# Other steps for the last-stage chunks, the weight scalings and half of block 0's last down products in a fused spectral filter and MLP

## The chip, the cores and the metric

The kernel runs on one core of one Trainium2 chip. The metric is device time in microseconds (us) from start to end of the program. TensorE (PE in the profile) does the matrix products, VectorE (DVE) and ScalarE (ACT) the elementwise work, GpSimd (POOL) some sums and its own DMA queue, SyncE (SP) most DMA issues. Each engine works through its own list in order and waits on semaphores for the others.

## The reference

For each of 8 batches, a sequence of 3008 tokens of width 256 is filtered in the frequency domain; then all 24064 tokens go through a two-layer MLP with a hard-swish between the layers, everything in float32:

```python
X = np.fft.rfft(x, axis=1)
Y = X * (filt_r + 1j * filt_i)[None]
y = np.fft.irfft(Y, n=3008, axis=1).reshape(24064, 256)
h = y @ w_in                      # 256 -> 2048
g = h * np.clip(h + 3, 0, 6) / 6
out = g @ w_out                   # 2048 -> 256
```

## The kernel before, in words

**The MLP is the frame.** The 24064 tokens are cut into 47 blocks of 512, held as 256 pairs (a sum half and a difference half of two tokens). Each block `k` takes 8 steps, `p` = 0 to 7, one for each 256 of the 2048 hidden columns. A step is numbered s = 8k + p. From block 1 on, both layers use a seven-product scheme (Strassen-like) on 2 by 2 blocks: a step has seven up products (`product`, L681) and the seven down products of the step before (`down`, L757), fourteen in place of sixteen. Block 0 uses plain products (`plain_up` L789, `plain_down` L800).

**The order inside a step** is written out by hand in the loop at L1093. TensorE gets: `up_1` (products A11, S1, A12), the step's early extra work, down 1, `up_2` (S2, S4), down 2 and 4, `up_3` (S3), down 5 and 6, `up_5` (A22), down 7 and 3. The two accumulators `al` and `be` in PSUM are used again and again: A22 needs `al` free, that is after VectorE's L712 has read it. ScalarE copies `al` and `be` out (L692, L693, L702, L721) and does two relus a step (`relu`, L726). VectorE does, in this order, the second hard-swish of the step before (`hswish(.., 1)`, L731), three sums of it (`g_sums`, L738, L739, L741), the additions L707 and L712, and the first hard-swish of the step (L731). At p = 0 of a block the outputs of the block before are collected (`out_1` on ScalarE, `out_2`, `out_3` on VectorE); at p = 1 follow `out_4` (two VectorE additions, L832 and L833, and one on GpSimd, L834) and `out_5` (L837), then the stores.

**The Fourier stages of later batches are placed into the steps of earlier blocks** by a plan: `at(step, fn, ...)` puts a function into a step. Functions of the tuple `EARLY` run right after `up_1`, all others at the end of the step. There are four stages: `a_unit` (first stage), `b_unit`, `f_unit`, `y_unit` and `bi_unit` (second stage: transform, multiplication with the filter on VectorE in L508 to L510, combination on VectorE in L519 and L520, inverse), and the last stage, `n_unit` and `n_five`. `n_five` takes a chunk of five frequencies of 47 pairs, 80 small matmuls (L621) into two PSUM tiles of the pool `psF`, which has just two buffers and serves all four stages. Then ScalarE copies them into the ring `xn` (L603), and if the chunk completes a block's 256 pairs, `ready` calls `t_sums`: seven GpSimd additions (L677) that make that block's `xt`, the inputs of its up products.

**Kinds of blocks.** For batch n from 2 on, the six blocks from `first[n] - 7` on get the letters c a A B A B. In blocks A and B the second stage runs: `f_unit` at steps 2, 3, 6, 7 of A and 4, 5 of B; `y_unit` at 4 and 5 of A and 2, 3, 6, 7 of B; `bi_unit` at 0 and 6 of B and at step 1 of the second A and of the block behind the last B. `FIVE_AT` says in which step of block k - 1 a chunk that begins in block k is made: for a block that holds the start of only one chunk, 4 in A, 2 in B. The DMA load of a chunk's inputs, `t4_load`, is placed one step behind the chunk that used the same half of the buffer.

**Block 1's weights.** Its sums of weight blocks are made on GpSimd (`w_sums`, L361) and two of them, S1 and A22, are multiplied by 2 and -2 in place by ScalarE (`w_scale`, L365), for p in step 7 + p, one step before `up_1` and `up_5` of block 1 use them.

**The end of block 0.** `plain_down` of p = 7 is done in step 8 (block 1, p = 0): sixteen matmuls between `up_4` and `up_5`, then `plain_out`, two ScalarE copies (L807) and the stores.

Of the kernel before, what the change touches and what calls it, by code (L numbers as in the profile page):

```python
# [33 lines left out]
D = 256  # L34
B = 8
# [146 lines left out]
def kernel(  # L182
# [482 lines left out]
    def xb(k, d, c):  # L665
        return xn[:, d, c, ts(k % 3, PAIRS)]
# [13 lines left out]
    def product(ps, p, w, x, start=False, stop=False):  # L680
        nc.tensor.matmul(ps, w_in[p][:, w, :], x, start=start, stop=stop, skip_group_check=True)  # L681
# [32 lines left out]
    def up_4(k, p):  # L714
        st["g", k, p] = gp.tile([P, 7, 256], FP32, name="g")
        relu(0)

    def up_5(k, p):
        al = st["up"][0]
        product(al, p, A22, xb(k, 1, 1), stop=True)  # L720
        nc.scalar.activation(out=st["h"][1][:, 0:256], in_=al, func=AXT.Copy)  # L721
        relu(1)

    def relu(i):
        r = rp.tile([P, 512], FP32, name="r", tag="r")
        nc.scalar.activation(out=r, in_=st["h"][i], func=AXT.Relu, bias=half_c, scale=1.0 / 6.0)  # L726
        st["r", i] = r
# [6 lines left out]
    def g_sums(k, p):  # L734
        hswish(k, p, 1)
        g = st["g", k, p]
        v = nc.vector
        v.tensor_tensor(out=g[:, G1, :], in0=g[:, G3, :], in1=g[:, G22, :], op=ALU.add)  # L738
        v.tensor_tensor(out=g[:, G3:G2 + 1:2, :], in0=g[:, G3:G1 + 1, :],  # L739
                        in1=g[:, G11:G11 + 1, :].broadcast_to([P, 2, 256]), op=ALU.subtract)  # L740
        v.tensor_tensor(out=g[:, G4, :], in0=g[:, G12, :], in1=g[:, G2, :], op=ALU.subtract)  # L741
# [19 lines left out]
    def last_down():  # L761
        p, v, add = NP - 1, nc.vector.tensor_tensor, ALU.add
        g, o = st["g", LAST, p], st["o", LAST][0]
        hswish(LAST, p, 1)
        ps = [psF.tile([P, 512], FP32, name="psf", tag="f") for t in range(2)]
        for i, a in ((0, G11), (1, G12)):
            for t in range(2):
                for u in range(2):
                    nc.tensor.matmul(ps[t][:, ts(u, D)], g[:, a + t, ts(u, P)],
                                     w_out[p][:, 2 * i:2 * i + 2, :].rearrange("p j m -> p (j m)"),  # L770
                                     start=i == 0 and u == 0, stop=i == 1, skip_group_check=True)
        out_4(LAST)
        v(out=o_at(LAST, 0, 1), in0=st["po", LAST][3][:, 1, :, :], in1=o_at(LAST, 0, 1), op=add)
        for t, qs in ((0, (nc.sync, nc.gpsimd, nc.scalar)), (1, (nc.sync, nc.scalar))):
            both = o[:, t, :, :].rearrange("p u d -> p (u d)")
            v(out=both, in0=ps[t], in1=both, op=add)
            store_last(t, qs)
# [6 lines left out]
    def plain_up(p):  # L784
        st["g", 0, p] = gp.tile([P, 7, 256], FP32, name="g")
        st["h"] = [psU.tile([P, 512], FP32, name=n) for n in ("al", "be")]
        for i in range(2):
            for d in range(2):
                nc.tensor.matmul(st["h"][i], w_in[p][:, 2 * d + i, :], xn[:, d, :, 0:PAIRS], start=d == 0, stop=d == 1)  # L789
            relu(i)  # L790
            hswish(0, p, i)

    def plain_down(p):
        g = st["g", 0, p]
        if p == 0:
            st["po", 0] = [psO.tile([P, 2, 2, P], FP32, name="po%d" % i) for i in range(2)]
        for t in range(2):
            for u in range(2):
                for i, a in ((0, G11), (1, G12)):
                    nc.tensor.matmul(st["po", 0][t][:, u, :, :].rearrange("p a m -> p (a m)"), g[:, a + t, ts(u, P)],  # L800
                                     w_out[p][:, 2 * i:2 * i + 2, :].rearrange("p j m -> p (j m)"),
                                     start=p == 0 and u == 0 and i == 0, stop=p == NP - 1, skip_group_check=True)

    def plain_out():
        st["o", 0] = op.tile([P, 2, 2, D], FP32, name="o", tag="o"), None
        for t, po in enumerate(st.pop(("po", 0))):
            nc.scalar.activation(out=st["o", 0][0][:, t, :, :].rearrange("p u d -> p (u d)"),  # L807
                                 in_=po.rearrange("p a u m -> p (a u m)"), func=AXT.Copy)
        store(0)
# [49 lines left out]
    def store(k):  # L859
        o = st["o", k][0]  # L860
        nc.sync.dma_start(o_d[ds(k * PAIRS, PAIRS)].rearrange("(u p) d -> p u d", p=P), o[:, 1, :, :])
        for u, p, m, b_, j, a in runs(k):
            for h in range(1 if j else 2):
                nc.sync.dma_start(raw(out, b_ * N + row(j, h, a), [[NC * D, m], [1, D]]), o[p:p + m, h, u, :])
        for b_, r, j, m, na in BACK.get(k, ()):
            to, half = out.offset + (b_ * N + N - j) * D, D // 2
            a0, a1 = ([[D, m], [-NC * D, na], [1, D]], [[NA * D, m], [D, na], [1, D]]) if m > 1 else (
                [[half, 2], [-NC * D, na], [1, half]], [[half, 2], [D, na], [1, half]])
            nc.sync.dma_start(bass.AP(tensor=out.tensor, offset=to, ap=a0),
                              bass.AP(tensor=o_d.tensor, offset=o_d.offset + r * D, ap=a1))  # L870
# [13 lines left out]
    plan = {}  # L884


    EARLY = (a_unit, b_unit, bi_unit, n_unit, n_five)

    def at(step, fn, *a):
        plan.setdefault((step, fn in EARLY), []).append((fn, a))  # L890

    with tc.manual_schedule():

# [113 lines left out]
        for i in range(2 * NP):  # L1007
            at(min(6 + i // 2, NP + 2), w_sums, i, int(i == gate), 4)
# [6 lines left out]
        n_at = {0: -2, 1: -2}  # L1015
        kinds = {}
        for n in range(2, B):
            for d, kind in enumerate("caABAB"):
                kinds[first[n] - 7 + d] = kind

        N_AT = {"c": ((6, 6), (3, 3), (6, 6)), "a": ((2, 4), (2, 4), (6, 6)), "A": ((4, 5), (1, 1), (4, 5)), "B": ((2, 3), (1, 1), (2, 3))}
        FIVE_AT = {"c": (6, 3, 6), "a": (4, 2, 4), "A": (4, 0, 4), "B": (2, 1, 3)}
        N_FIRST = {0: ((3, 4),), 1: ((), (2, 2), (3, 3)), 2: ((1, 1),), 3: ((1, 1),)}
        in_block = {}
        for i in range(2, len(chunks)):
# [2 lines left out]
        for i in range(2, len(chunks)):  # L1028
# [3 lines left out]
            at_, kind = same.index(i) + 1 if len(same) > 1 else 0, kinds.get(k - 1, "a")  # L1032
            steps = N_FIRST[k - 1][at_] if k - 1 in N_FIRST else (FIVE_AT[kind][at_],) * 2 if len(chunks[i][1]) == NJ else N_AT[kind][at_]
            if head and len(same) == 1:
# [58 lines left out]
        for i in range(len(items) + 1):  # L1093
            up = i < len(items)
            k, p = items[min(i, len(items) - 1)]
            dn = i > 0
            kd, pd = items[i - 1]
            def do(early):
                for fn, a in plan.get((i, early), ()):
                    fn(*a)  # L1100

            if k == 0:
                plain_up(p)
                do(True)
                if dn:
                    plain_down(pd)
                do(False)
                continue
            if not up:
                last_down()  # L1110
                break
            up_1(k, p)
            ends = k == LAST and p == NP - 1
            do(True)
            last_plain = dn and kd == 0
            dn = dn and kd > 0
            if dn:
                g_sums(kd, pd)
                down(kd, pd, 1)
            if up:  # L1120
                up_2(k, p)
            if dn and pd == 0 and kd > 1:
                out_4(kd - 1)
            if up:
                up_2b(k, p)
            if dn:
                down(kd, pd, 2, 4)
                if pd == NP - 1:
                    out_1(kd)
            if up:  # L1130
                up_3(k, p)
            if dn:
                down(kd, pd, 5, 6)
            if up:
                up_4(k, p)
            if ends:
                out_1(k)
            if last_plain:
                plain_down(pd)
                plain_out()  # L1140
            if dn and pd == 0 and kd > 1:
                out_5(kd - 1)
            if up:
                hswish(k, p, 0)
            if up:
                up_5(k, p)
            if dn:
                if pd == NP - 1 or ends:
                    out_2(kd)
                down(kd, pd, 7, 3)  # L1150
                if pd == NP - 1 or ends:
                    out_3(kd)
            do(False)


# [28 lines left out]
```

## Time and profile before

| what | value |
|---|---|
| median of 3 runs | 2675.4 us (2675.08 to 2677.41) |
| the profiled execution's own time | 2675.01 us |
| span in the profile | 2673.2 us |
| PE busy | 2646.0 us, 99% |
| DVE busy | 2064.2 us, 77% |
| ACT busy | 1303.9 us, 49% |
| POOL busy | 510.3 us, 19% |
| granted clock | 0.999 |

The times between the starts of the first product (A11) of one step and of the next, from the timeline:

| steps | length, us |
|---|---|
| with the up and down products only (146 of 169) | 6.15 |
| with `n_five` (29 of 45) | 7.66 |
| with `a_unit` (48 of 49) | 7.37 |
| with `bi_unit` of step 1 in the second A, or with `b_unit` | 7.36 to 7.37 |
| step 4 of A, with `n_five` (12) | 7.75 to 7.76 |
| step 5 of A, products only (12) | 6.87 to 6.89 |
| step 3 of B, products only (9) | 6.87 to 6.88, once 7.10 |
| steps 8 to 15 (block 1) | 8.85, 7.90, 8.03, 8.23, 7.38, 7.38, 6.52, 7.38 |

Busy shares are averages over the whole span. The modelled ends of matmuls make PE look busy where it waits, so a wait is better seen in the length of a step.

### The profile page before, as it was taken

Reading aid. Unit: us, or ns where it says so; the run is one execution under the profiler, and the core shown is the slowest. Engines: PE = TensorE matmul, PEld = TensorE weight load, DVE = VectorE, ACT = ScalarE, POOL = GpSimd, SP = SyncE. Lnnn points to the kernel's source line nnn. Section 1 sums busy time; section 2 is a strip of 40 time slices with the busy share of each in tenths; the row PEclk is TensorE's granted clock in tenths of the full one; section 3 lists DMA queues with packets and bytes.
Section 4 is the critical chain, followed back from the end, with each engine's and each line's share of the span. In section 5 each row is a group of like instructions: output and inputs, shape, how many; then the busy total and the mean of one; then the engine's idle time right before and its main releaser. Section 6 shows DMA issues by size and latency. Waiting matters only on the chain.

```text
span 2673.2 us, 54258 instructions
## 1 busy us (share of the span) xinstructions
PE 2646.0 (99%) x21584; PEld 2316.2 (87%) x21584; DVE 2064.2 (77%) x3503; ACT 1303.9 (49%) x2672; POOL 510.3 (19%) x731
## 2 busy tenths in 40 slices
PE   9999999999999999999999999999999999999999
PEld 6588888888888888888888888888888888899998
DVE  7978867887678876788767887678886888767666
ACT  4444444445444445445454545545445454454554
POOL 2242122111221112211131111311112111111110
PEclk9999999999999999999999999999999999999999
DMA  9732233212332123311233112231123321110000
GB/s 255 206 95 70 61 105 96 64 38 66 90 103 61 41 65 88 109 56 40 70 84 109 56 41 75 79 108 56 41 74 79 108 59 39 52 42 18 23 20 24
DMA packets 134818, 198.24 MB, mean 74 GB/s; under 512 B 23146, under 2 KB 99016, under 8 KB 134374
## 3 DMA queue, kind: packets, MB, share of 16 engines
q1 hardware_dynamic: 117037, 150.12, 19.8%
q0 software_dynamic: 16960, 44.16, 6.3%
q8 instruction: 170, 2.79, 0.4%
q14 instruction: 82, 0.67, 0.1%
q10 hardware_dynamic: 569, 0.50, 0.1%
HBM read 122.43 MB, written 83.98 MB: 77 GB/s over the span
## 4 chain that ended last, share of the span: by engine, by line
PE 89%; DVE 9%; issue 1%; ACT 1%; DMA 0%; POOL 0%; SPq 0%; DVEq 0%; POOLq 0%; ACTq 0%
PE po L757 40%; PE al L681 22%; PE be L681 17%; PE psn L621 2%; PE psf L531 2%; PE psf L440 2%; DVE g L731 2%; PE psf L487 1%; DVE y L519 1%; DVE y L520 1%; DVE g L738 1%; DVE h L707 1%; DVE h L712 1%; DVE g L739 1%; DMA w_all<-in_x_dram 0%
## 5 line engine op out<-in xcount | busy, mean ns | idle before, releaser
L757 PEld LDWEIGHTS po<-w_all,g 128*128 128x128 f32 x10276 | 1361.2, 191 | 154.6 <-issue 44.1
L757 PE MATMUL po<-w_all,g 128*128 128x128 f32 x10276 | 1402.6, 277 | 0.4 <-DVE g L731 0.2
L726 ACT ACTIVATE r<-h,half_c 128x512 f32<-128x512 f32 x736 | 531.0, 721 | 362.9 <-DVE h L707 350.8
L731 DVE SCALAR_TENSOR_TENSOR g<-r,h 128x512 f32<-128x512 f32 x736 | 526.9, 716 | 209.5 <-ACT r L726 195.7
L681 PE MATMUL al<-xt,w_all 128*128 128x256 f32 x2208 | 659.8, 381 | 0.8 <-POOL w_all L361 0.6
L681 PE MATMUL be<-xt,w_all 128*128 128x256 f32 x1472 | 437.9, 379 | 0.0
L707 DVE TENSOR_TENSOR h<-be,s 128x512 f32<-128x512 f32 x368 | 253.8, 690 | 167.3 <-PE be L681 162.6
L681 PEld LDWEIGHTS al<-xt,w_all 128*128 128x128 f32 x2208 | 335.3, 192 | 1.9 <-POOL w_all L361 1.5
L681 PEld LDWEIGHTS be<-xt,w_all 128*128 128x128 f32 x1472 | 279.7, 190 | 37.8
L721 ACT ACTIVATE h<-al 128x256 f32<-128x256 f32 x368 | 141.0, 383 | 326.8 <-PE al L681 326.8
L712 DVE TENSOR_TENSOR h<-al,s 128x256 f32<-128x256 f32 x368 | 155.7, 423 | 154.3 <-PE al L681 153.1
L739 DVE TENSOR_TENSOR g<-g 128x512 f32<-128x512 f32 x367 | 255.6, 696 | 12.6
L677 POOL TENSOR_TENSOR xt<-xn 128x256 f32<-128x256 f32 x184 | 145.3, 809 | 539.7 <-ACT xn L603 539.7
L702 ACT ACTIVATE s<-al 128x256 f32<-128x256 f32 x368 | 141.1, 383 | 194.9 <-PE al L681 191.3
L681 PE MATMUL al<-xn,w_all 128*128 128x256 f32 x736 | 222.5, 384 | 10.4 <-DVE h L712 10.4
L693 ACT ACTIVATE s<-be 128x256 f32<-128x256 f32 x368 | 141.1, 383 | 178.6 <-PE be L681 178.6
L681 PE MATMUL be<-xn,w_all 128*128 128x256 f32 x736 | 219.7, 380 | 1.0 <-ACT w_all L365 0.5
L738 DVE TENSOR_TENSOR g<-g 128x256 f32<-128x256 f32 x367 | 172.3, 469 | 12.5
L547 POOL DMA_DIRECT2D g_tmp<-t x96 | 55.4, 591 | 656.7 <-ACT t L534 644.3
L692 ACT ACTIVATE s<-al 128x256 f32<-128x256 f32 x368 | 140.9, 383 | 68.5 <-PE al L681 68.5
L741 DVE TENSOR_TENSOR g<-g 128x256 f32<-128x256 f32 x367 | 160.0, 436 | 12.5
L461 POOL DMA_DIRECT2D z_tmp<-t x192 | 95.1, 503 | 364.6 <-DVE t L454 347.4
(149 smaller groups left out, 1867.3 us busy)
## 6 DMA issues: line engine op xcount, KB each, us to landing
g_tmp<-t POOLq DMA_DIRECT2D x96, 256.0 KB, 3.7
t<-g_tmp SPq DMA_DIRECT2D x184, 120.0 KB
t<-z_tmp SPq DMA_DIRECT2D x42, 512.0 KB
z_tmp<-t POOLq DMA_DIRECT2D x192, 96.0 KB, 2.5
xs<-in_x_dram SPq DMA_DIRECT2D x112, 128.0 KB
o_tmp<-o SPq DMA_DIRECT2D x46, 256.0 KB
ft<-in_filt_r_dram SPq DMA_DIRECT2D x168, 64.0 KB
ft<-in_filt_i_dram SPq DMA_DIRECT2D x168, 64.0 KB
```

The lines of the kernel that those rows point to most:

```text
L677: nc.gpsimd.tensor_tensor(out=o, in0=x0, in1=x1, op=op_)
L681: nc.tensor.matmul(ps, w_in[p][:, w, :], x, start=start, stop=stop, skip_group_check=True)
L693: nc.scalar.activation(out=s5, in_=be[:, 1, :], func=AXT.Copy)
L702: nc.scalar.activation(out=s[:, 1, :], in_=al, func=AXT.Copy)
L707: nc.vector.tensor_tensor(out=st["h"][0].rearrange("p (a n) -> p a n", a=2), in0=be, in1=s, op=ALU.add)
L712: nc.vector.tensor_tensor(out=st["h"][1][:, 256:512], in0=al, in1=s5, op=ALU.add)
L726: nc.scalar.activation(out=r, in_=st["h"][i], func=AXT.Relu, bias=half_c, scale=1.0 / 6.0)
L731: nc.vector.scalar_tensor_tensor(out=st["g", k, p][:, o:o + 2, :].rearrange("p a n -> p (a n)"), in0=st["r", i], scalar=1.0, in1=st["h"][i ...
L738: v.tensor_tensor(out=g[:, G1, :], in0=g[:, G3, :], in1=g[:, G22, :], op=ALU.add)
L739: v.tensor_tensor(out=g[:, G3:G2 + 1:2, :], in0=g[:, G3:G1 + 1, :], in1=g[:, G11:G11 + 1, :].broadcast_to([P, 2, 256]), op=ALU.subtract)
L741: v.tensor_tensor(out=g[:, G4, :], in0=g[:, G12, :], in1=g[:, G2, :], op=ALU.subtract)
L757: nc.tensor.matmul(st["po", k][bank][:, part, u, :], g[:, a, ts(u, P)], w_out[p][:, w, :], start=(p == 0 and n in OPENS and u == 0), stop= ...
```

## The change

Three parts, all in the order of work; no instruction is added or taken away.

1. `FIVE_AT`: in A the chunk is made in step 1 in place of 4, in B in 1 in place of 2, and the second A of each six becomes a new kind D, with step 0 in place of 4. Chunks of blocks that hold two chunk starts, and all other kinds, stay. This moves 20 chunks: in A from steps 52, 100, 148, 196, 244, 292 to 49, 97, 145, 193, 241, 289; in D from 68, 116, 164, 212, 308 to 64, 112, 160, 208, 304; in B from 58, 74, 106, 122, 154, 170, 202, 218, 250 each to the step before. With them move their copies, the `t_sums` behind them, and for some later chunks the `t4_load`, up to four steps earlier.
2. `w_scale` gets a place of its own: after `up_4` (the first relu) in mid-step, no longer at the step's end.
3. `plain_down` of block 0's p = 7 is split: the matmuls of token half 0 stay ahead of `up_5`, those of half 1 and `plain_out` go behind it.

```diff
-    def plain_down(p):
+    def plain_down(p, tokens=(0, 1)):
...
-        for t in range(2):
+        for t in tokens:
...
-        plan.setdefault((step, fn in EARLY), []).append((fn, a))
+        plan.setdefault((step, 0 if fn in EARLY else 1 if fn == w_scale else 2), []).append((fn, a))
...
-            for d, kind in enumerate("caABAB"):
+            for d, kind in enumerate("caABDB"):
...
-        N_AT = {"c": ((6, 6), (3, 3), (6, 6)), "a": ((2, 4), (2, 4), (6, 6)), "A": ((4, 5), (1, 1), (4, 5)), "B": ((2, 3), (1, 1), (2, 3))}
-        FIVE_AT = {"c": (6, 3, 6), "a": (4, 2, 4), "A": (4, 0, 4), "B": (2, 1, 3)}
+        N_AT = {"c": ((6, 6), (3, 3), (6, 6)), "a": ((2, 4), (2, 4), (6, 6)), "A": ((4, 5), (1, 1), (4, 5)), "B": ((2, 3), (1, 1), (2, 3)), "D": ((4, 5), (1, 1), (4, 5))}
+        FIVE_AT = {"c": (6, 3, 6), "a": (4, 2, 4), "A": (1, 0, 4), "B": (1, 1, 3), "D": (0, 0, 4)}
...
             if up:
                 up_4(k, p)
+                do(1)
             if ends:
                 out_1(k)
             if last_plain:
-                plain_down(pd)
-                plain_out()
+                plain_down(pd, (0,))
...
             if up:
                 up_5(k, p)
+            if last_plain:
+                plain_down(pd, (1,))
+                plain_out()
...
-            do(False)
+            do(2)
```

In block 0 the three places follow one another: early, then `plain_down`, then the scalings, then the rest.

More of the change, by code (lines that the diff above doesn't have):

```diff
@@ L1097, with do @@
             kd, pd = items[i - 1]
-            def do(early):
-                for fn, a in plan.get((i, early), ()):
+            def do(place):
+                for fn, a in plan.get((i, place), ()):
                     fn(*a)
@@ L1103 @@
                 plain_up(p)
-                do(True)
+                do(0)
                 if dn:
                     plain_down(pd)
-                do(False)
+                do(1)
+                do(2)
                 continue
@@ L1113 @@
             ends = k == LAST and p == NP - 1
-            do(True)
+            do(0)
             last_plain = dn and kd == 0
@@ L1135 @@
                 up_4(k, p)
+                do(1)
             if ends:
@@ L1152 @@
                     out_3(kd)
-            do(False)
+            do(2)
 _INS = ['x', 'filt_r', 'filt_i', 'moe_w_in', 'moe_w_out']
```

## The prediction

> **What bounds the kernel now.** I read the page first, then the chain of work that ended last.
>
> ```profile
> span 2673.2 us, 54258 instructions
> ...
> PE 89%; DVE 9%; issue 1%; ACT 1%; DMA 0%; POOL 0%; SPq 0%; DVEq 0%; POOLq 0%; ACTq 0%
> ```
>
> TensorE carries 89% of the chain, so only time in which it waits can be won. VectorE's 9% says that it is made to wait. The longest pieces of the chain show where:
>
> ```profile
> 1122.62 1.11 DVE y L519
> 1123.75 1.12 DVE y L520
> 1124.96 1.04 DVE g L731
> 1164.26 1.11 DVE y L519
> ```
>
> The trio L519, L520, L731 comes back once for each slow step 5 of A and 3 of B, always with 1.0 to 1.1 us where the same instruction takes 0.69 elsewhere. The timeline of steps 148 and 149 (block 18, A, steps 4 and 5; start, duration, engine, instruction) shows why:
>
> ```profile
> 1115.82 0.60 PE L681 MATMUL al<-xt,w_all 128*128 128x256 f32 x2
> ...
> 1122.00 2.30 POOL L677 TENSOR_TENSOR xt<-xt 128x256 f32<-128x256 f32 x2
> ...
> 1122.62 1.10 DVE L519 TENSOR_TENSOR y<-s 64x512 f32<-64x512 f32 x1
> ...
> 1123.58 0.60 PE L681 MATMUL al<-xt,w_all 128*128 128x256 f32 x2
> ...
> 1123.75 1.10 DVE L520 TENSOR_TENSOR y<-s 64x512 f32<-64x512 f32 x1
> ...
> 1124.96 1.03 DVE L731 SCALAR_TENSOR_TENSOR g<-r,h 128x512 f32<-128x512 f32 x1
> ...
> 1128.56 0.41 DVE L712 TENSOR_TENSOR h<-al,s 128x256 f32<-128x256 f32 x1
> ...
> 1129.03 0.70 PE L681 MATMUL al<-xn,w_all 128*128 128x256 f32 x2 [0.46 <-DVE h L712]
> ...
> 1130.45 0.60 PE L681 MATMUL al<-xt,w_all 128*128 128x256 f32 x2
> ```
>
> The chunk of step 148 sets GpSimd's `t_sums` going 4.0 us into the step; they run into the `y_unit` that VectorE has at its end. L519, L520, L731 and L738 each lose 0.35 to 0.41 us, 1.57 together, so L712 is late and A22 waits. Step 149 takes 1130.45 - 1123.58 = 6.87 us, not the 6.15 of an undisturbed one. Step 148 itself takes 7.76, not 7.66: its chunk waits about 0.1 us for PSUM tiles that `f_unit` of step 147 still reads (L510 until 1117.26).
>
> The scalings have a wait of their own (steps 11 and 12):
>
> ```profile
> 160.48 0.72 ACT L726 ACTIVATE r<-h,half_c 128x512 f32<-128x512 f32 x1
> 161.11 0.49 ACT L365 ACTIVATE w_all<-w_all 128x128 f32<-128x128 f32 x2
> ...
> 161.46 0.30 PEld L681 LDWEIGHTS be<-xn,w_all 128*128 128x128 f32 x2 [0.50 <-ACT w_all L365]
> ```
>
> The S1 product is the second of its step and waits for weights that ScalarE scales only after the second relu.
>
> **What the Trainium skill says.** "SBUF — State Buffer", section "Who interferes with whom": a VectorE instruction with two SBUF inputs contends with a GpSimd instruction that reads SBUF; one with at most one SBUF input, outside two-port modes, doesn't. The trace agrees: under `t_sums` L519 goes from 0.69 to 1.10 us, L738 from 0.42 to 0.83, L739 from 0.69 to 1.10, while L707 and L712, with one input in PSUM, stay at 0.69 and 0.42. The same page, "SBUF: two separate sides", calls it an exclusive lock, held for a whole instruction by whichever came first; that fits the fixed additions of about 0.4 us. "TensorE: Matmul & The Clock Gate", "The mechanism", says matmuls run strictly in order: a late A22 holds every product behind it, as in step 149.
>
> **Part 1, the 20 chunks.** Removed: at the 11 chunks of A and D the excess of step 4 over 7.657 (sum 1.09 us) and of step 5 over 6.148 (sum 8.06); at the 9 of B that of step 3 over 6.148 (sum 6.80, of which I leave out 0.22, since block 7's step 3 has an S3 that is late for a reason I can't name). Together 15.73 us. The chunk's work (80 matmuls, two to four copies, seven sums) moves whole, so step 4 loses the same 1.51 us that step 0 or 1 gains.
>
> Added: what the sums hit at the new place. They start 3.9 us into the chunk's step (like 2439.94 in step 340, begun at 2436.0) and last 6.0 us: 2.2 us into the next step. There they slow L731 and L738. Step 341, products only behind a chunk, took 6.148 all the same, but its L712 ended 4.62 into the step and A22 started at 4.82; in step 149 A22 started 0.06 after L712. So about 0.14 us of cover is left.
>
> In A and B the chunk now lies in step 1, and `out_4`'s GpSimd addition L834 queues behind the sums, into step 2. One place has that already, steps 17 and 18:
>
> ```profile
> 205.99 0.60 PE L681 MATMUL al<-xt,w_all 128*128 128x256 f32 x2
> ...
> 207.51 0.83 DVE L738 TENSOR_TENSOR g<-g 128x256 f32<-128x256 f32 x1
> 208.03 0.91 POOL L834 TENSOR_TENSOR o<-p,o 128x256 f32<-128x256 f32 x1
> 208.38 1.10 DVE L739 TENSOR_TENSOR g<-g 128x512 f32<-128x512 f32 x1
> 209.52 0.42 DVE L741 TENSOR_TENSOR g<-g 128x256 f32<-128x256 f32 x1
> ```
>
> L739 loses 0.41 too. Step 18 hides that under other matmuls. Step 2 of B has none: 0.41 less the 0.14 of cover leaves a stall of 0.27; I take 0.26, 9 times, 2.34 us. Bounds: 0 if L834 falls beside L707, 0.7 (all that is lost today) if a fourth sum is hit. Step 2 of A has 1.22 us of `b_unit` matmuls ahead of A22: nothing. The `y_unit` at the end of step 2 of B then runs alone, 2 x 0.69, and L707 of step 3 should start about 3.5 in; step 341 started it at 3.61 unharmed.
>
> In D the sums reach into step 1, which has 1.22 us of `bi_unit` matmuls; its L707 has 0.5 us of idle ahead of it and may start 0.9 late before A22 does; L731 and L738 lose 0.8. Nothing; 0.3 each if that cover is thinner. Step 256 shows a chunk at such a step 0 at 7.657, though without sums.
>
> Step 1 of A and B: VectorE has no idle time before L707 there today (0 in step 57), but `n_five` stands ahead of down 1, so PE reaches S4 1.5 us later, before the sums have begun. PSUM tiles: step 0 of A has no user of `psF`, `bi_unit`'s copies of step 0 of B end within it, D follows one that ended in step 6. Nothing.
>
> Queues. SP: the `t4_load`s (four issues, 1.60 us) come up to four steps earlier and still lie at least 10 steps ahead of their chunk. The stores of a block wait on SP for L834, in A and B now some 6 us later, and behind them stand the loads of the next steps; the earliest use of one of them (the filter table loaded in step 4 of A) is eight steps after it. POOL: the inverse's stores in step 1 of D stand behind the sums, done 2.2 us into that step, before the copies they store. Nothing on either.
>
> **Part 2, the scalings.** Steps 9 to 15 exceed what their contents cost elsewhere (7.370, 7.657, 7.657, 7.011, 7.011, 6.148, 7.011) by 0.53, 0.37, 0.57, 0.37, 0.37, 0.37, 0.37: 2.95 us. In mid-step ScalarE idles 0.97 to 1.13 us before L721, and two scalings take 0.49, so they fit. They also need the sums of their p: those of p = 1 end at 131.93, the relu ahead of the scaling at 132.84; later ones have more room. In step 7 a weight conversion's absolute value slips behind the scalings by 1 us, to 127.7, and is used at 129.38. Gain 2.95; if a sum were late, ScalarE would hold L721, between 0 and 2.95.
>
> **Part 3, the split.** In step 8 S3 starts at 131.43, then come sixteen matmuls of 0.216 and A22; L721 sits behind a `plain_out` copy, and A11 of step 9 starts at 136.60. With eight matmuls behind A22, L721 and relu run under them: 131.43 + 0.43 + 16 x 0.216 + 0.43 = 135.75. Gain 0.85; L712 (ends 132.55) is done before A22 at 133.6. The copies end about 136.5, before down 1 of step 9 (138) needs their PSUM; the next L692 slips by 0.1 us, under `a_unit`. At worst 0.3.
>
> **Sum.** 15.73 - 2.34 + 2.95 + 0.85 = 17.2 us. Span 2673.2 - 17.2 = 2656.0. The profiled execution took 2675.01, 1.8 around its span, and the median of the runs is 0.4 above it: 2658.2.
>
> **The rivals.** *The contention follows the sums:* 0.7 at each step 2 of B and 0.3 at each step 2 of A and step 1 of D: 15.73 - 6.3 - 3.3 + 3.8 = 9.9 gained, 2665.5. For it: VectorE gets no lighter, and step 341 has 0.14 us left. Against: step 18 shows the cost of L834, and `y_unit` is out of reach. *The scalings wait for their sums* in mid-step and win nothing: 2661.1. GpSimd works on them without a pause from 123.8 to 160.8, but ahead of need. *Nothing moves:* VectorE's lost time comes back whole at the new place, 0.7 to 0.8 for each chunk, and only parts 2 and 3 stay, half of them: about 2673. *Slower:* the chunk, now in front of down 1 in step 0 or 1, waits for its `psF` tiles or its loaded inputs, and all products stand behind it. Twenty chunks at x us against 19.5 gained: even at 0.98 each, slower by over 0.2% (5.4 us) from 1.25; at 1.5 it gives 2686. Against it: step 256 and step 17 show no wait of that sort.
>
> **How the numbers follow.** Forecast 0.62, the following contention 0.18, waiting scalings 0.10, nothing moves 0.05, slower 0.05. The first case's own range is 2655 to 2661 (stall of step 2 of B from 0 to 0.5). The range goes from 2654.5 (all hidden, and block 7's 0.22 won) to 2667, which takes in the second and third; outside are the last two and some edges. A change of 0.2%, 5.4 us, is about what a measurement can tell from none. Faster by more: 0.90, within: 0.05, slower by more: 0.05.
>
> **What would show it.** Step 4 of A and D and step 2 of B at 6.15, the new chunk steps at 7.66, step 5 of A and 3 of B at 6.15, L519 and L520 at 0.69 there; step 2 of B at 6.3 to 6.5 with L739 at 1.10 beside L834; step 2 of A and 1 of D at 7.37; steps 9 to 15 at the lengths named; step 8 near 8.0. Wrong would be a wait of L621 on `psF`, L707 late in step 1, or L365 waiting for L361.

## The result and the profile after

The changed kernel takes 2661.78 us (median of four runs, 2660.12 to 2664.24) against 2675.95 before: ratio 0.9947, 95% interval 0.993 to 0.9964, so 14.2 us less. The forecast was 2658.2 within 2654.5 to 2667. The profiled execution took 2661.05 us with a span of 2659.2, 14.0 less than the one before.

The page of the changed kernel, its span and the chain that ended last:

```profile
span 2659.2 us, 54237 instructions
...
PE 95%; DVE 3%; DMA 1%; issue 0%; ACT 0%; SPq 0%; POOL 0%; POOLq 0%; DVEq 0%; ACTq 0%
```

VectorE's share of the chain falls from 9% to 3%. Among the longest pieces of the chain (start, duration, what) the trio that begins with a slow L519 is left at two places, where it stood at 21:

```profile
262.90 1.12 DVE y L519
...
1887.68 1.11 DVE y L519
```

The first belongs to batch 1, whose stages the change doesn't touch; the second to block 32, whose chunk in step 4 stayed.

**Where the time went, step by step** (time between the starts of A11; the sums are over all steps of the kind that changed):

| steps | before, us | after, us | sum of the change, us |
|---|---|---|---|
| 20 new chunk steps (step 0 of D, 1 of A and B) | 6.15, once 6.21 | 7.66 | +30.1 |
| step 4 of A and D (11) | 7.75 to 7.76 | 6.34 to 6.35 | -15.6 |
| step 5 of A and D (11) | 6.87 to 6.89 | 6.15 | -8.1 |
| step 2 of B (9) | 7.66 | 6.24 to 6.46 | -11.6 |
| step 3 of B (9) | 6.87 to 6.88, once 7.10 | 6.15 | -6.8 |
| step 8 | 8.85 | 8.07 | -0.78 |
| steps 9 to 15 | 52.82 together | 49.86 | -2.95 |

All steps from 8 on together are 15.5 us shorter. (A step that a change doesn't touch, step 9 aside, differs by less than 0.03 us between two profiles; over all steps such differences add up to as much as 0.4 us.) The span is only 14.0 shorter, because step 8 begins at 129.30 us and not at 127.75; more on that at the end of the experiments.

The timeline of step 148 (block 18, A, step 4; start, duration, engine, instruction) no longer has a chunk, and still isn't 6.15 long:

```profile
1110.14 0.60 PE L681 MATMUL al<-xt,w_all 128*128 128x256 f32 x2
...
1110.89 0.69 DVE L510 TENSOR_TENSOR s<-psf,ft 64x512 f32<-64x512 f32 x1
...
1111.61 0.69 DVE L731 SCALAR_TENSOR_TENSOR g<-r,h 128x512 f32<-128x512 f32 x1
...
1113.98 0.69 DVE L707 TENSOR_TENSOR h<-be,s 128x512 f32<-128x512 f32 x1
...
1115.06 0.70 PE L681 MATMUL al<-xn,w_all 128*128 128x256 f32 x2
...
1116.48 0.60 PE L681 MATMUL al<-xt,w_all 128*128 128x256 f32 x2
```

L510, the end of `f_unit` of step 3, runs 1.4 us into the step; only then comes the hard-swish L731, and L707 starts 3.84 us in. The product A22 (`al<-xn`) starts 4.92 us in; in an undisturbed step it starts at 4.82. The step takes 6.34 us. Step 149, which lost 0.72 us to the sums before, takes 6.15.

Step 154 (block 19, B, step 2) of the same kernel shows the stall that was forecast:

```profile
1151.26 0.60 PE L681 MATMUL al<-xt,w_all 128*128 128x256 f32 x2
...
1153.28 0.90 POOL L834 TENSOR_TENSOR o<-p,o 128x256 f32<-128x256 f32 x1
1153.63 1.10 DVE L739 TENSOR_TENSOR g<-g 128x512 f32<-128x512 f32 x1
...
1156.18 0.70 PE L681 MATMUL al<-xn,w_all 128*128 128x256 f32 x2
...
1157.61 0.60 PE L681 MATMUL al<-xt,w_all 128*128 128x256 f32 x2
```

L834 stands behind the sums, L739 takes 1.10 us, and the step 6.35.

The scalings of step 11 lie in ScalarE's gap now, and step 12's S1 product starts without a wait:

```profile
157.51 0.72 ACT L726 ACTIVATE r<-h,half_c 128x512 f32<-128x512 f32 x1 [0.84 <-DVE h L707]
158.14 0.49 ACT L365 ACTIVATE w_all<-w_all 128x128 f32<-128x128 f32 x2
159.36 0.38 ACT L721 ACTIVATE h<-al 128x256 f32<-128x256 f32 x1 [0.73 <-PE al L681]
...
160.49 0.59 PE L681 MATMUL be<-xn,w_all 128*128 128x256 f32 x2
```

### The profile page after: what moved, and what is told of

Same layout as the page of the kernel before. It is cut to its first block, busy times and chain, and to the rows that moved or that the text cites. A ratio compares the mean times of both kernels' runs of the same rounds, so it can differ in the third digit from the quotient of the medians.

```text
span 2659.2 us, 54237 instructions
## 1 busy us (share of the span) xinstructions
PE 2642.1 (99%) x21584; PEld 2317.6 (87%) x21584; DVE 2058.6 (77%) x3503; ACT 1306.3 (49%) x2672; POOL 495.1 (19%) x731
## 4 chain that ended last, share of the span: by engine, by line
PE 95%; DVE 3%; DMA 1%; issue 0%; ACT 0%; SPq 0%; POOL 0%; POOLq 0%; DVEq 0%; ACTq 0%
PE po L757 43%; PE al L681 24%; PE be L681 18%; PE psn L621 2%; PE psf L531 2%; PE psf L440 2%; PE psf L487 1%; DVE g L731 1%; DMA w_all<-in_x_dram 0%; PE po L496 0%; PE po L800 0%; PE psn L632 0%; PE psf L496 0%; PE po L407 0%; DVE y L332 0%
## 5 line engine op out<-in xcount | busy, mean ns | idle before, releaser
L731 DVE SCALAR_TENSOR_TENSOR g<-r,h 128x512 f32<-128x512 f32 x736 | 531.3, 722 | 212.6 <-ACT r L726 200.3
L707 DVE TENSOR_TENSOR h<-be,s 128x512 f32<-128x512 f32 x368 | 253.9, 690 | 158.5 <-PE be L681 151.2
L712 DVE TENSOR_TENSOR h<-al,s 128x256 f32<-128x256 f32 x368 | 155.9, 424 | 150.2 <-PE al L681 149.1
L739 DVE TENSOR_TENSOR g<-g 128x512 f32<-128x512 f32 x367 | 261.4, 712 | 12.6
L702 ACT ACTIVATE s<-al 128x256 f32<-128x256 f32 x368 | 141.4, 384 | 194.5 <-PE al L681 191.1
L677 POOL TENSOR_TENSOR xt<-xn 128x256 f32<-128x256 f32 x184 | 135.8, 756 | 434.4 <-ACT xn L603 434.4
L738 DVE TENSOR_TENSOR g<-g 128x256 f32<-128x256 f32 x367 | 172.5, 470 | 12.5
```

The costliest lines, as they stand in the source:

```text
L702: nc.scalar.activation(out=s[:, 1, :], in_=al, func=AXT.Copy)
L707: nc.vector.tensor_tensor(out=st["h"][0].rearrange("p (a n) -> p a n", a=2), in0=be, in1=s, op=ALU.add)
L712: nc.vector.tensor_tensor(out=st["h"][1][:, 256:512], in0=al, in1=s5, op=ALU.add)
L731: nc.vector.scalar_tensor_tensor(out=st["g", k, p][:, o:o + 2, :].rearrange("p a n -> p (a n)"), in0=st["r", i], scalar=1.0, in1=st["h"][i ...
```

## The experiments

**The parts one by one.** The theory is the prediction's sum, part for part; the rival is that the parts depend on one another.

Except for those that are timed below, each kernel of an experiment was run once, so these are compared by their steps.

Part 1 alone: the three lines with `caABDB`, `N_AT` and `FIVE_AT` on the kernel before.

> Only the 20 chunks move (part 1). My theory: steps 8 to 15 keep their lengths of before (8.85, 7.90, 8.03, 8.23, 7.38, 7.38, 6.52, 7.38 us), the steps of blocks A, B and D are those of the changed kernel (step 5 of A and 3 of B 6.15, step 2 of B 6.24 to 6.46, step 4 of A and D 6.34), and the lengths of all steps from 8 on add up to 11.8 us less than before. Rival (the parts help one another): the sum differs from 11.8 by more than 0.5 us.

Measured: the steps from 8 on are 11.64 us shorter, steps 8 to 15 are those of before, the steps of A, B and D those of the changed kernel. Part 1 stands by itself.

Part 2 alone:

```diff
-        plan.setdefault((step, fn in EARLY), []).append((fn, a))
+        plan.setdefault((step, 0 if fn in EARLY else 1 if fn == w_scale else 2), []).append((fn, a))
...
                 up_4(k, p)
+                do(1)
```

> Only the scalings move to mid-step (part 2). My theory: steps 9 to 15 lose 0.53, 0.37, 0.57, 0.37, 0.37, 0.37, 0.37 us, together 2.95, step 8 stays near 8.85, all others as before. Rival (the scalings wait for GpSimd's sums and hold ScalarE in mid-step): ScalarE waits at L365 for L361, and steps 8 to 15 lose less than 2 us.

Measured: steps 9 to 15 lose 0.46, 0.37, 0.57, 0.37, 0.37, 0.37, 0.37, together 2.88 us; step 8 is unchanged. (Over all steps the difference is 2.45, since small differences elsewhere add 0.43.) ScalarE isn't held in these steps: L365 waits for L361 once in all, 1.06 us in step 7, and step 7 takes no longer for it (8.11 us). The rival with waiting scalings falls.

Part 3 alone:

```diff
             if last_plain:
-                plain_down(pd)
-                plain_out()
+                plain_down(pd, (0,))
...
                 up_5(k, p)
+            if last_plain:
+                plain_down(pd, (1,))
+                plain_out()
```

> Only half of block 0's last down products moves behind A22 (part 3). My theory: step 8 loses 0.78 to 0.85 us, but since the scalings then stand behind the two copies out of PSUM at the end of step 8, step 9's S1 product waits longer than before and gives back about 0.35: steps 8 and 9 together lose about 0.5 us. Rival (the parts are independent): steps 8 and 9 together lose 0.8 us.

Measured: step 8 is 0.78 us shorter, step 9 is 0.18 longer, together 0.60 less. The truth lies between the two numbers, nearer to the first: the split alone gives something back to the scalings behind it. Parts 2 and 3 alone sum to 3.48, in the changed kernel steps 8 to 15 lose 3.74; so 0.26 us comes only from having both.

**Are the sums the cause?** On the kernel before the chunks keep their steps, but their sums wait, by a small addition that reads the result of the second `y_unit`:

```diff
-        st["y", b, i] = y
+        st["y", b, i] = st["ylast"] = y
...
-        ready(i)
+        if sums:
+            ready(i)
+
+    def sums_behind_y(i):
+        y = st["ylast"]
+        nc.gpsimd.tensor_tensor(out=wait_c, in0=y[:, 1, 0:8], in1=y[:, 1, 8:16], op=ALU.add)
+        ready(i)
...
+        for s, i in behind:
+            at(s, sums_behind_y, i)
```

> The kernel before, chunks in their old steps, but the seven GpSimd sums of a chunk made in step 4 of A or 2 of B wait for the second y_unit (one small GpSimd addition that reads its result is put ahead of them). My theory (the sums slow VectorE): step 5 of A falls from 6.88 to 6.15 and step 3 of B to 6.15, with L519 and L520 at 0.69; step 4 of A stays 7.75; the sums now meet steps 6 of A and 4 of B, whose b_unit covers most of it, and the inverse in steps 0 and 6 of B waits up to 0.4 us longer than its 0.09. Rival (VectorE is late from f_unit and y_unit alone, the sums only happen to be there): step 5 of A and 3 of B stay at 6.87 or more.

The timeline of steps 149 and 150 of this kernel (its lines stand further down: L520 is L519 of before, L521 is L520, L688 are the up products, L684 the sums):

```profile
1122.18 0.69 DVE L520 TENSOR_TENSOR y<-s 64x512 f32<-64x512 f32 x1
...
1123.14 0.60 PE L688 MATMUL al<-xt,w_all 128*128 128x256 f32 x2
...
1129.29 0.60 PE L688 MATMUL al<-xt,w_all 128*128 128x256 f32 x2
...
1129.82 0.20 POOL L631 TENSOR_TENSOR wait_c<-y 128x8 f32<-128x8 f32 x1 [29.99 <-DVE y L521]
```

Step 149 takes 1129.29 - 1123.14 = 6.15 us, with VectorE's work and its order unchanged and only GpSimd's sums later. All twelve steps 5 of A and nine steps 3 of B do the same; step 4 of A stays at 7.75 (one 7.99). So the sums are the cause, and the rival falls. The lost time comes back in part: steps 7 of A and 5 of B are 0.17 to 0.18 us longer (one 0.45), steps 0 and 6 of B, where `bi_unit` waits for `psF`, 0.22 to 0.24. In all the steps are 6.1 us shorter, less than the 11.6 that moving the chunks gives.

**Step 2 of B.** In the changed kernel, where a chunk is made in step 1 its sums are issued in mid-step, behind L834:

```diff
-        plan.setdefault((step, 0 if fn in EARLY else 1 if fn == w_scale else 2), []).append((fn, a))
+        plan.setdefault((step, 0 if fn in EARLY else 1 if fn in (w_scale, ready) else 2), []).append((fn, a))
...
-                at(s1, n_five, i)
+                mid = s1 % NP == 1 and k > 4
+                at(s1, n_five, i, not mid)
+                if mid:
+                    at(s1, ready, i)
```

> The changed kernel, but where a chunk is made in step 1 its seven GpSimd sums are issued in mid-step, behind the addition L834 of out_4 and not ahead of it. My theory (L834 behind the sums hits L739 of step 2 and costs it 0.41 us): step 2 of B, now 6.24 to 6.46, falls to 6.15 to 6.20 with L739 at 0.69; all step lengths together 1.5 to 2.0 us less than in the changed kernel. Rival (the sums alone make step 2 late, wherever L834 is): step 2 of B stays above 6.24.

The timeline of steps 153 and 154 (the lines of this kernel that come after `n_five` stand one further down: L835 is L834, L740 is L739):

```profile
1146.46 0.73 POOL L835 TENSOR_TENSOR o<-p,o 128x256 f32<-128x256 f32 x1 [5.76 <-DVE o L833]
...
1150.74 0.60 PE L682 MATMUL al<-xt,w_all 128*128 128x256 f32 x2
...
1153.33 0.69 DVE L740 TENSOR_TENSOR g<-g 128x512 f32<-128x512 f32 x1
...
1156.89 0.60 PE L682 MATMUL al<-xt,w_all 128*128 128x256 f32 x2
```

The addition now ends before the sums begin, L739 takes 0.69, and the step 6.15 us. The nine steps together lose 1.91 us, all steps 1.75 (step 9 took 0.22 longer, for the reason given under "A wait that hadn't been seen"). The theory holds.

**Step 4 of A and D.** In the changed kernel the second `f_unit` moves one step later, with the two `y_unit`s on other steps:

```diff
-                                 for p in ((2, 3, 6, 7, 12, 13), (4, 5, 10, 11, 14, 15), (8, 14, 17)))
+                                 for p in ((2, 4, 6, 7, 12, 13), (3, 5, 10, 11, 14, 15), (8, 14, 17)))
...
-"D": (0, 0, 4)}
+"D": (0, 0, 5)}
```

> The changed kernel, but in blocks A and D the second f_unit of the first pair moves from step 3 to 4 and its two y_units from steps 4 and 5 to 3 and 5 (and block 32's second chunk from step 4 to 5, since its PSUM tiles are held until then). My theory (step 4 of A and D is 0.19 us late because two f_units at the ends of steps 2 and 3 leave VectorE behind, and the chunk that gave it time is gone): step 4 of A and D falls from 6.34 to 6.15, step 5 stays 6.15; eleven times 0.19 = 2.1 us less. Rival (it is something else in step 4): step 4 stays at 6.34.

The timeline of step 148 of this kernel:

```profile
1108.29 0.69 DVE L519 TENSOR_TENSOR y<-s 64x512 f32<-64x512 f32 x1
...
1108.82 0.60 PE L681 MATMUL al<-xt,w_all 128*128 128x256 f32 x2
...
1112.06 0.68 DVE L707 TENSOR_TENSOR h<-be,s 128x512 f32<-128x512 f32 x1
...
1114.97 0.60 PE L681 MATMUL al<-xt,w_all 128*128 128x256 f32 x2
```

With one `y_unit` ahead in place of an `f_unit`, L707 starts 3.24 us in and the step takes 6.15. The eleven steps lose 2.1 us, and block 32 another 0.65. So the 0.19 us was VectorE's backlog from two `f_unit`s on two steps.

**Both together, timed.**

> Both of the foregoing together on the changed kernel. My theory: they add up, 3.6 to 4.1 us less than the changed kernel, about 2658 us. Rival: one gives the other's gain back, less than 2 us.

> The changed kernel once more, for the comparison on the same chip: 2660 to 2664 us; the start of step 8 between 129 and 130.5 us into the span, as in the other profiles but the first.

Measured on one chip, with 2676.48 us for the kernel before: both 2655.29 us (2654.99 to 2659.23), ratio 0.9926, interval 0.9914 to 0.9939; the changed kernel 2660.34 (2660.22 to 2662.13), ratio 0.994, interval 0.9926 to 0.9954. So against the kernel before on the same chip the change is worth 16.1 us here, where the first comparison gave 14.2 and the steps 15.5. Both edits together win 5.05 us more by the medians, 4.3 by the steps of their profiles: more than the forecast 3.6 to 4.1, because block 32 adds 0.65. The gains add up, and this version is ahead of both kernels; the two intervals overlap a little, the single runs don't overlap.

Step 8 of the repeated changed kernel began at 128.94 us, just outside the expected 129 to 130.5.

**A wait that hadn't been seen.** In the repeated changed kernel step 9 took 8.79 us and not 7.37. Its timeline:

```profile
138.06 0.42 SPq L269 DMA_DIRECT2D ft<-in_filt_i_dram  x1
...
138.58 1.56 SPq L461 DMA_DIRECT2D z_tmp<-t  x4
...
142.06 0.60 ACT L443 ACTIVATE t<-psf 128x512 f32<-128x512 f32 x1 [3.17 <-DMA z_tmp<-t]
142.55 0.38 ACT L702 ACTIVATE s<-al 128x256 f32<-128x256 f32 x1
...
143.07 0.67 PE L681 MATMUL al<-xt,w_all 128*128 128x256 f32 x2 [1.18 <-POOL w_all L361]
```

The first-stage results stand on SP behind sixteen issues for two filter tables. L443 waits for their buffer, L702 stands behind it, and S3 needs L702's copy; the GpSimd instruction that the profile names for S3 isn't what it waited for. That the delay comes from L443 can be read from six profiles with the table loads in their old place. Where L443 waited 1.43 and 1.63 us for `z_tmp`, step 9 took 7.37; with waits of 1.89, 1.97, 2.10 and 3.17 it took 7.50, 7.59, 7.71 and 8.79: beyond the slack, each tenth of wait is a tenth of step. Moving the second table's loads from step 6 to step 10:

```diff
-                s = f_at[2 * (c - FB) + 1] + 1 if c >= FB else a_at[-1 if n > 1 else 3] + 1
+                s = f_at[2 * (c - FB) + 1] + 1 if c >= FB else a_at[-1 if n > 1 or c else 3] + 1
```

> Both of the foregoing, and the eight load issues of batch 1's second filter table move from step 6 to step 10. My theory (in step 9 ScalarE's copy L443 waits for first-stage results that stand on SP behind sixteen table issues, and after step 8 got shorter this reaches TensorE in some executions, by 0.2 to 1.4 us): L443 of step 9 no longer waits for the z_tmp transfer, step 9 takes 7.37 us, the median is 0 to 1 us lower than without it, and the runs lie closer together. Rival (the scatter of step 9 comes from the transfer itself): step 9 is over 7.4 us in this profile or the scatter stays.

> The two foregoing edits without the table's move, for the comparison on the same chip: 2655 to 2659 us, step 9 between 7.37 and 8.8 us.

The timeline with the table moved:

```profile
133.85 1.57 SPq L461 DMA_DIRECT2D z_tmp<-t  x4
...
141.09 0.60 ACT L443 ACTIVATE t<-psf 128x512 f32<-128x512 f32 x1 [0.65 <-PE psf L440]
```

L443 waits for its matmuls alone and step 9 takes 7.37 us, in this one profile. But the times are 2657.12 (2655.22 to 2657.84) against 2656.68 (2655.31 to 2657.97) without the move: no gain that can be measured, and the scatter stays. The mechanism in step 9 holds; that it makes the scatter of the runs isn't borne out.

**The stretch ahead of step 8.** Its start was at 127.75 us in the profile before, 129.30 after, and in the other ten profiles at 128.70 to 131.92. Part 1 alone and the postponed sums have exactly the work of before up to there, and begin step 8 at 129.41 and 129.35. The first load of `x`, before any product, held the chain for 12.00 us in the profile before and 13.12 in the one after. The difference is there in full at the first product of block 0:

```profile
63.71 1.98 PE L789 MATMUL al<-xn,w_all 128*128 128x512 f32 x4 [0.30 <-ACT xn L661]
```

```profile
65.27 1.98 PE L789 MATMUL al<-xn,w_all 128*128 128x512 f32 x4 [0.30 <-ACT xn L661]
```

The first line is from the kernel before, the second from the changed one. The change alters nothing ahead of step 7, and step 7 takes 8.11 us in all twelve profiles. So the 1.55 us by which the span fell short of the steps is no part of the change. What makes those loads take longer in one execution than in another stays open.

## Why the prediction was right, and where not

**What bounded the kernel** and the cause of the slow steps were read rightly: with the sums out of the way of `y_unit`, the 20 steps behind the chunks' old places are all at 6.15 us, 14.86 us won where 14.64 was counted. The rest is the 0.22 us of block 7's step 3, which the prediction couldn't explain. The kernel before shows what it was:

```profile
499.14 0.60 PE L681 MATMUL al<-xt,w_all 128*128 128x256 f32 x2
...
501.06 1.03 DVE L731 SCALAR_TENSOR_TENSOR g<-r,h 128x512 f32<-128x512 f32 x1
...
502.14 1.16 PE L757 MATMUL po<-w_all,g 128*128 128x128 f32 x8 [0.23 <-DVE g L731]
...
503.13 0.60 PE L681 MATMUL al<-xt,w_all 128*128 128x256 f32 x2
```

VectorE is later there than elsewhere, and the down products ahead of S3 wait 0.23 us for the slowed hard-swish L731, which makes the operand of down 2. The postponed sums took this away too: that step fell from 7.10 to 6.15. So it is the sums again. In this step the chain runs over L731 alone, so the trio L519, L520, L731 doesn't come back at every slow step, as the prediction says, but at all except this one (and once in batch 1).

**Step 2 of B** was forecast at 0.26 us of stall each, 2.34 together, from L834 behind the sums and 0.14 us of cover. Measured 0.10 to 0.31, together 2.02, and the edit that puts L834 first takes it away.

**The step that failed** is in the count of what part 1 removes: "The chunk's work ... moves whole, so step 4 loses the same 1.51 us that step 0 or 1 gains", and with it the whole 1.09 us of excess. The chunk's matmuls in step 4 had been the time in which VectorE worked off the two `f_unit`s of steps 2 and 3. With them gone step 4 stands 0.19 us above 6.15: 2.13 us over eleven steps. I had read only the 0.1 us that the chunk waited there for `psF`, not what it hid. The need for cover could have been read in the kernel before: in step 147, behind the first `f_unit`, VectorE came to L707 without a pause (3.42 us in) and just in time, and a second `f_unit` followed.

**Steps 8 to 15**: 3.80 counted, 3.74 measured. The wait of L443 cost step 9 nothing in the first profile and 1.42 us in another. That is more than part 3 won, so "at worst 0.3" was too narrow; that the shorter step 8 exposes this wait is argued, not shown.

**Sum**: 17.2 counted; less 2.13 for step 4, plus 0.32, 0.22 and small remainders, gives the 15.5 us that the steps show. That is 1.7 of the 3.6 us between forecast and median. Another 1.55 is the earlier start of step 8 in the profile from which the forecast was made, and 0.3 is that the median lies 0.7 above the profiled run, where 0.4 was counted. The range was drawn for other cases and had no term for either, so that it holds the result is in part luck.

**The rivals.** The contention did follow the sums, but at 0.22 us for each step 2 of B and nothing in step 2 of A or 1 of D, not the 0.7 and 0.3 of that case. No movement and the slower case didn't come, nor did scalings that win nothing: one wait of L365 for L361, named as a sign of being wrong, did show in step 7 (0.94 us), where it cost no time. `n_five` had no wait on `psF` at its new places, where each step takes 7.66.

## What to carry to other kernels

Measure the length of each step of a regular kernel, group the steps by content, and look at those that are longer than their content: here this gave nearly every microsecond, where busy shares of 99% gave none. Before moving work out of a step, ask what runs under it on the other engines: its time is also their cover. Where GpSimd adds while VectorE has operations with two inputs in SBUF, place the sums where VectorE reads PSUM (L707 and L712 kept their 0.69 and 0.42 us) or has time.

## What the runs showed of the hardware

The lost time comes mostly in pieces of about 0.41 us: L519 takes 0.69 us alone and 1.10 under a GpSimd addition; L739 mostly 0.69 or 1.10, L738 mostly 0.42 or 0.83. In step 148 of the kernel before, the first additions of a chunk meet L707, which reads PSUM, and the next ones L731, L519 and L520, which don't:

```profile
1119.83 2.10 POOL L677 TENSOR_TENSOR xt<-xn 128x256 f32<-128x256 f32 x3 [19.56 <-ACT xn L603]
1120.31 0.69 DVE L707 TENSOR_TENSOR h<-be,s 128x512 f32<-128x512 f32 x1 [0.68 <-PE be L681]
...
1122.00 2.30 POOL L677 TENSOR_TENSOR xt<-xt 128x256 f32<-128x256 f32 x2
```

An addition takes 0.70 us in the first group and 1.15 in the second: both engines are slowed. The prediction called the fixed losses a fit to a lock that is held for a whole instruction. In kind they fit, for the loss is the same for short and long instructions; in size they don't. If each kept the other out for its whole time, one addition and one L519 would take 0.70 + 0.69 = 1.39 us together; but L520 starts 1.13 us after L519, with one addition begun between them. So the two overlap in part; how, the runs don't show.

Steps that nothing touched, step 9 aside, repeat within 0.03 us from one execution to the next, while the loads ahead of step 8 moved its start over 4.2 us: a comparison by steps resolved 0.1 us in a step where the runs' times could not.
